# One queue for the planner's transfers, joint loads of q and k, and another source and time for the second weight matrix's sums

## The chip, the cores and the metric

The kernel runs on one core of one Trainium2 chip. The metric is the device time of one execution in microseconds (us), lower is better. TensorE (PE) multiplies matrices, VectorE (DVE) and ScalarE (ACT) work element by element, GpSimd (POOL) makes the maxima and sums over partitions. Transfers between the core's memory and DRAM are started by three of the queues: SP, which does nothing else, ACT, which also computes, and POOL. Each engine takes its instructions strictly in the order in which they stand. In the built program every transfer started by SP or ACT is given one of eight semaphores, in the order of the program and over both queues together; before it is started, the transfer that had the same semaphore last must have landed. A queue that waits for that also holds what stands behind it.

## The reference

Attention over 8 batches, 8 heads and 576 positions, each query seeing the 64 positions up to its own, and behind it a two-layer network (leaky slope 0.01) on the 4608 tokens:

```python
# q, k, v: (8, 8, 576, 64) float32; w_in: (512, 2048), w_out: (2048, 512)
scores = scale * np.matmul(q, k.transpose(0, 1, 3, 2))
mask = (rel >= 0) & (rel < 64)               # rel = query position - key position
scores = np.where(mask, scores, -1000000000.0)
attn = softmax(scores)
x = np.matmul(attn, v).transpose(0, 2, 1, 3).reshape(4608, 512)
h = x @ w_in
g = np.maximum(0.01 * h, h)
return g @ w_out
```

## The kernel before

Tokens are handled in pairs of 64-row query blocks, 36 pairs in all; `m` counts them. Every float32 product is made of three matmuls on a value's rounded part (hi) and what the rounding left (lo): hi*hi, hi*lo, lo*hi. The weights arrive as 64-bit numbers and become float32 on the chip. There are 32 half-tiles `n` (even: w_in, odd: w_out) for 16 tiles `f`; each goes through `raw` (a 512 KB load, L205, from ACT), `bits`, `sign`, `abs`, `clamp`, `join` (float32 in `singles[n]`), `chi` (`split`, L239: the hi part, and the float32 half-tile to DRAM, `w_single`, L241) and `rest` (the lo part, L245).

The work has three parts.

1. **The list** `ORDER` (L51 to 79), 0 to about 131 us. It is written out by hand: pairs 0 to 7, and the network's first products (`M`, L425, with `lk`, `gh`, `gl` for the leaky step and the split into hi and lo; `W`, L461) on the first 1024 tokens with tiles 0 to 7. All engines follow this one order. `ev` stores a finished sum.
2. **The walk**, about 131 to 357 us: the rest of the first 1536 tokens. 32 units `n`, each a product of 12 matmuls (L880), a leaky step (L894) and the cast to hi (L897) on ACT, the lo part on DVE (L900), and 12 matmuls into the sums (L889), which stand on PE two units behind the product. Beside it the pairs 8 to 19 are attended, the weights' raw parts are stored in DRAM (`store`, L632, 256 KB each), and sums of weight parts are prepared (`prepare`, L968) for the next part.
3. **The stages** `s` = 0, 1, 2, from 357 us, 1024 tokens each. The first layer is done in seven products in place of eight (`m`, L1058), for which `x_build` (L808) makes sums of attention rows and `prepare(0, ...)` sums of parts of w_in. The second layer is plain in stage 0 (`y`, L1083, in two halves) and in seven products in stages 1 and 2 (`z`, L1121). Weights come in 1 MB pieces on POOL's queue (`fill`, L1042) from two DRAM tensors, `w_first` and `w_second`. The last pairs, 20 to 35, are attended during stage 0 and at the start of stage 1.

From the walk on, the order is made by a planner, `arrange` (L524): each operation has an engine, an assumed duration, what it must come after, and a rank; the planner plays them through and notes the order in which they would start. `load` puts a transfer on SP, `bulk` puts one on ACT. The order on each engine is then fixed.

One pair's way through the engines: PE makes the scores (`S`, L272); DVE masks them (L657); POOL makes the maximum (L672); DVE subtracts it (L679); ACT takes the exponential (L683); POOL adds up (L675, 3.3 us each); a small transfer brings the sums to 128 partitions (`late_c`, L686, two of 2 KB); ACT adds a small number (`guard`, L690) and DVE inverts; two more transfers spread the inverse (`rows`, L697, and `late_r`, L710); DVE multiplies (`late_n`, L733); a last one stores the rows (`x_rows`, L736). q, k and v of a later pair are loaded by ACT (L161, L165, L169).

`prepare(n, f, ...)` loads parts of tiles f and f+8, makes sums and differences of their quarters (L979), splits them into hi (ACT, L982) and lo (DVE, L985), and stores them (L989 for w_out, into `w_second`; L992 for w_in, into `w_first`). Loads and stores of it stand on ACT:

```python
got = [bulk(partial(fetch, i), *freed, *all_in, rank=hurry + 0.1) for i in range(2)]
...
prepared[n, f] = [bulk(partial(keep, i), lo, rank=hurry + 0.1) for i in range(2)]
```

Finished sums leave the accumulators by copies that alternate between DVE and ACT (`early_out` L912, `put_out` L1086).

Of the kernel before, what the change touches and what calls it, by code (L numbers as in the profile page):

```python
# [38 lines left out]
PACE = 2  # L39
EARLY = 20  # L40
# [27 lines left out]
bits17 join16 sign17 L7 abs17 clamp17 join17 bits18 raw19 chi16 ev0 chi17 ev1 raw20 rest16 sign18 abs18 rest17 M11  # L68
bits19 clamp18 M12 lk11 gh11 gl11 lk12 gh12 sign19 join18 M13 W11 M14 gl12 abs19 raw21 chi18 lk13 bits20 clamp19
join19 chi19 raw22 sign20 rest18 rest19 W12 M15 gh13 gl13 abs20 W13 bits21 clamp20 sign21 join20 bits22 abs21 lk14  # L70
sign22 clamp21 join21 raw23 chi20 M16 gh14 gl14 W14 rest20 raw24 abs22 clamp22 join22 chi21 raw25 bits23 rest21 sign23
bits24 lk15 chi22 gh15 gl15 sign24 abs23 abs24 clamp23 join23 bits25 chi23 raw26 lk16 M17 W15 clamp24 sign25 rest22
join24 M18 abs25 gh16 raw27 clamp25 gl16 rest23 join25 W16 chi24 rest24 bits26 sign26 lk17 chi25 rest25 raw28 abs26
gh17 bits27 clamp26 gl17 sign27 join26 abs27 clamp27 join27 chi26 lk18 chi27 gh18 bits28 sign28 rest26 gl18 k8 q8 v8
W17 q9
# [27 lines left out]
def band_attention_ffn(ctx: ExitStack, tc: tile.TileContext, qT, kB, vW, vL, w_in, w_out, eye_mask, out, outT):  # L103
# [37 lines left out]
    qs = [const.tile([P, UNITS, NP, QB], F32, name=f"q{i}") for i in range(2)]  # L141
    ks = [const.tile([P, UNITS, NP, QB], F32, name=f"k{i}") for i in range(2)]
# [16 lines left out]
    def load_q(m, queue=nc.sync):  # L159
        if m < NU // 2:  # L160
            queue.dma_start(q_of(m), qT[m])  # L161

    def load_k(m, queue=nc.sync):
        if m < NU // 2:
            queue.dma_start(k_of(m), kB[m])  # L165
# [24 lines left out]
    w_single = dram.tile([2 * FT, P, 512], F32, name="w_single")  # L190
# [48 lines left out]
    def split(n):  # L239
        nc.scalar.copy(flat(parts(n)[0]), singles[n])  # L240
        nc.scalar.dma_start(w_single[n], singles[n])  # L241
# [238 lines left out]

    def idle(n):
        ps = bank("h", f"idle{next(count)}")
        for _ in range(n):
            nc.tensor.matmul(ps, wi[half + 4][0][:, 0], flat(wi[half + 4][0]), start=True, stop=True)

    def begin(k):
# [6 lines left out]
        ev=lambda k: due.pop(0)(),  # L493
    )
    nc.vector.memset(flat(wi[half + 4][0]).bitcast(F32), 0.0)
    nc.scalar.dma_start(k_of(0), kB[0])
# [24 lines left out]
    def bulk(fn, *after, rank=1.0):  # L521
        return op("ACT", 0.45, fn, *after, rank=rank, lag=1.5, land=6.0)

    def arrange():  # L524
# [9 lines left out]
        order = []  # L534
        while any(waiting.values()):
# [76 lines left out]
    for name in late.split():  # L612
# [3 lines left out]
        if kind == "raw":  # L616
            o["raw"] = bulk(partial(fetch_w, n), weights_of.get(n - 3, {}).get("join"), rank=0.2)
            continue
# [11 lines left out]

    def store(to, f, *cut):
        nc.sync.dma_start(to, both[f][cut])  # L632

    stored = []
    for f in turn_of:
        near, far = f % half, f // half
        for a, k in ((0, 0), (256, 4)) if far == 0 else ((256, 5),):
            to = first_at(near, k).rearrange("p (i c) -> p i c", i=2)
            stored.append((f, partial(store, to, f, slice(None), slice(2), slice(a, a + 256))))
        for a in range(2):  # L640
            to = second_at[:, (0, 2)[far] + (6, 2)[far] * a, near].rearrange("p (i c) -> p i c", i=2)
            stored.append((f, partial(store, to, f, slice(None), slice(2, 4), slice(256 * a, 256 * a + 256))))


# [63 lines left out]
    def spread_of(m, j):  # L708
        row = rows[m : m + 1, 512 * j : 512 * j + 512]
        nc.sync.dma_start(later["r"][64 * j : 64 * j + 64], row.broadcast_to([64, 512]))  # L710
# [41 lines left out]
    def attend(m, gate):  # L752

        o, late = at.setdefault(m, {}), 0.0 if early(m) else 0.5
        before, two, three = (at.get(m - i, {}) for i in (1, 2, 3))
        if m > PAIRED:
            if m > PAIRED + 1:
                o["q"] = bulk(partial(load_q, m, nc.scalar), two["S"], rank=0.5 + late)
            o["k"] = bulk(partial(load_k, m, nc.scalar), before["S"], rank=0.2 + late)
            o["v"] = bulk(partial(load_v, m, nc.scalar), before["X1"])  # L760
        takes = [before["take"], two["take"]] if m == EARLY else []
        if held_back(m - 1) and before:
            takes += [before["B0"], before["B1"]]
        o["S"] = op(
            "PE", 1.0, partial(scores_of, m), o.get("q"), o.get("k"), before.get("E1"), before.get("E0"), three.get("take"), *takes, s_free,
# [15 lines left out]
    def normalise(m):  # L781
# [11 lines left out]
        spread = [load(partial(spread_of, m, j), o["rows"], before.get("Y"), rank=0.3 + late) for j in range(2)]  # L793
# [21 lines left out]
    def x_build(s, n, xt_of, xt_free, x_free):  # L815
# [13 lines left out]
        def fetch(i):  # L829
            nc.sync.dma_start(xt_of()[0][:, 512 * i : 512 * (i + 1)], x_rows[m + i])  # L830

        got = [load(partial(fetch, i), *at[m + i]["kept"], *xt_free, rank=urge) for i in range(2)]
# [85 lines left out]
    def second_step(n):  # L918
# [5 lines left out]
        if n in ends:  # L924
            evicted[c] = []
            for i in range(4):
                engine = "DVE" if c == 1 or c == 0 and i < 2 or i % 2 == 0 else "ACT"
# [39 lines left out]
    def prepare(n, f, at, hurry, *freed):  # L967
        def prep(i):  # L968
            return (g_tile(at) if at else hold("spare", F32)).rearrange("p (k i c) -> p k i c", k=4, i=2)[:, :, i]
# [4 lines left out]
        def fetch(i):  # L974
            to = prep(0)[:, i::2] if n else prep(0)[:, 2 * i : 2 * i + 2]
            nc.scalar.dma_start(to, w_single[2 * (f + half * i) + n].rearrange("p (k c) -> p k c", k=2))
# [10 lines left out]
        def keep(i):  # L987
            if n:
                nc.scalar.dma_start(second_at[:, 1::2, f, 256 * i : 256 * i + 256], prep(i))  # L989
            else:  # L990
                a, b, k = ((0, 3, 1), (3, 4, 6))[i]
                nc.scalar.dma_start(  # L992
                    first_at(f, k, b - a), (g_tile(at) if at else hold("spare", F32))[:, 512 * a : 512 * b]
                )

        got = [bulk(partial(fetch, i), *freed, *all_in, rank=hurry + 0.1) for i in range(2)]
        d1 = op("DVE", 0.5, partial(join_of, 2, (0, 2), (0, 3), ALU.add), *got, rank=hurry, lag=2.0)
        d3 = op("DVE", 0.5, partial(join_of, 1, (0, 0), (0, 2), ALU.subtract), *got, rank=hurry, lag=2.0)
        d2 = op("DVE", 0.5, partial(join_of, 0, (1, 2), (0, 0), ALU.subtract), d1, rank=hurry)
        d4 = op("DVE", 0.5, partial(join_of, 3, (0, 1), (1, 0), ALU.subtract), d2, rank=hurry)  # L1000
        hi = op("ACT", 1.07, high, d1, d2, d3, d4, rank=hurry)
        lo = op("DVE", 1.4, low, hi, rank=hurry)
        prepared[n, f] = [bulk(partial(keep, i), lo, rank=hurry + 0.1) for i in range(2)]
# [6 lines left out]
    for f in range(half):  # L1010
        prepare(1, f, 0, OUT_PREP + 0.1 * f, *used_last[0])
# [73 lines left out]
    def put_out(s, t, i, o):  # L1085
        (nc.scalar.copy if i % 2 else nc.vector.tensor_copy)(o(), tiles[i])  # L1086
# [280 lines left out]
```

## Time and profile before

| | |
|---|---|
| median of 3 runs | 886.56 us (884.72 to 1079.68) |
| the profiled execution | 888.97 us, its span 887.2 us |
| weight load PEld busy | 690.0 us (78%), beside PE |
| DMA bytes over the span | 227.08 MB, mean 256 GB/s |
| of these on POOL's queue / ACT's / SP's | 90.18 / 77.31 / 58.51 MB |
| attention sums on POOL (L675) | 56 of 3.3 us |

A row of the timeline gives start, duration, engine, line, operation, output and inputs, how many instructions were merged, and in brackets the idle time just before and what ended it. ACTq and SPq are the queues' starts of transfers; a transfer's bytes move after that. PEclk is TensorE's granted clock as a share of full speed; "DMA" shares are of the sixteen DMA engines' time. The stretch table gives, for each stretch, its length, each engine's busy time with its count of instructions, PEclk, the DMA share and GB/s.

### The profile page before, as it was taken

Reading aid. Unit: us, or ns where it says so; the run is one execution under the profiler, and the core shown is the slowest. Engines: PE = TensorE matmul, PEld = TensorE weight load, DVE = VectorE, ACT = ScalarE, POOL = GpSimd, SP = SyncE. Lnnn points to the kernel's source line nnn. Section 1 sums busy time; section 2 is a strip of 40 time slices with the busy share of each in tenths; the row PEclk is TensorE's granted clock in tenths of the full one; section 3 lists DMA queues with packets and bytes.
Section 4 is the critical chain, followed back from the end, with each engine's and each line's share of the span. In section 5 each row is a group of like instructions: output and inputs, shape, how many; then the busy total and the mean of one; then the engine's idle time right before and its main releaser. Section 6 shows DMA issues by size and latency. Waiting matters only on the chain.

```text
span 887.2 us, 16927 instructions
## 1 busy us (share of the span) xinstructions
PE 853.5 (96%) x6778; PEld 690.0 (78%) x6778; DVE 631.6 (71%) x891; ACT 376.0 (42%) x620; POOL 364.2 (41%) x218
## 2 busy tenths in 40 slices
PE   8999999999999997999999899989999999999998
PEld 5776888888777776888887678767888888888886
DVE  7889885768579864875776989466578864545863
ACT  4655554333333333544453534253354523334431
POOL 5323000958768720677776777663000100000000
PEclk9999999999999998999999999989999999999999
DMA  9875876786899997799999998976856776666662
GB/s 342 265 233 184 275 219 240 234 302 207 276 292 336 314 317 273 245 299 356 309 295 317 295 300 266 344 235 207 276 195 214 236 242 210 194 191 197 199 222 87
DMA packets 103742, 227.08 MB, mean 256 GB/s; under 512 B 17008, under 2 KB 47856, under 8 KB 94704
## 3 DMA queue, kind: packets, MB, share of 16 engines
q0 software_dynamic: 14432, 90.18, 31.5%
q10 hardware_dynamic: 41712, 77.31, 26.3%
q1 hardware_dynamic: 47520, 58.51, 20.3%
q8 instruction: 53, 0.87, 0.4%
q14 instruction: 25, 0.20, 0.1%
HBM read 168.59 MB, written 57.26 MB: 255 GB/s over the span
## 4 chain that ended last, share of the span: by engine, by line
PE 48%; DMA 12%; DVE 9%; issue 3%; ACT 1%; SPq 1%; ACTq 0%; POOL 0%; DVEq 0%
PE m L1058 25%; PE z L1121 17%; DMA w_second<-p 2%; DMA late_r<-rows 2%; DMA w_second<-pspare 2%; DMA rows<-late_c 2%; DMA x_rows<-late_n 1%; PE y L1083 1%; PE acc L889 1%; DMA p<-x_rows 1%; PE s L272 1%; PE o L722 1%; DMA outT<-p 1%; DVE p L835 1%; DVE gs L1076 1%
## 5 line engine op out<-in xcount | busy, mean ns | idle before, releaser
L1058 PE MATMUL m<-pfew,p 128*128 128x512 f32 x720 | 171.5, 393 | 0.8 <-DVE pxa L1067 0.7
L1058 PEld LDWEIGHTS m<-pfew,p 128*128 128x128 f32 x720 | 134.8, 189 | 30.2 <-DVE pxa L1067 1.1
L1042 POOL DMA_DIRECT2D p<-w_second x44 | 26.3, 597 | 143.0 <-PE z L1121 98.8
L889 PE MATMUL acc<-p,gs 128*128 128x512 f32 x324 | 79.8, 394 | 0.0
L1042 POOL DMA_DIRECT2D p<-w_first x42 | 22.8, 542 | 134.0 <-PE m L1058 78.6
L1058 PE MATMUL m<-pxb,p 128*128 128x512 f32 x288 | 72.1, 397 | 5.0 <-ACT p L1070 5.0
L672 POOL PARTITION_ALL_REDUCE g<-late_f x20 | 37.0, 1894 | 96.1 <-DVE late_f L657 71.6
L675 POOL PARTITION_ALL_REDUCE late_o<-late_f x20 | 65.5, 3283 | 20.5 <-ACT late_f L683 12.3
L1067 DVE TENSOR_TENSOR p<-m,pxa 128x512 f32<-128x512 f32 x60 | 41.3, 688 | 41.9 <-PE m L1058 41.6
L1067 DVE TENSOR_TENSOR pxa<-m,pxa 128x512 f32<-128x512 f32 x60 | 41.3, 689 | 41.0 <-PE m L1058 38.0
L889 PEld LDWEIGHTS acc<-p,gs 128*128 128x128 f32 x324 | 60.1, 188 | 13.0
L1070 ACT ACTIVATE p<-p 128x512 f32<-128x512 f32 x60 | 37.9, 631 | 74.2 <-DVE p L1067 74.1
L1058 PEld LDWEIGHTS m<-pxb,p 128*128 128x128 f32 x288 | 54.4, 191 | 17.3 <-ACT p L1070 5.4
L880 PE MATMUL h<-pxa,p 128*128 128x512 f32 x228 | 58.4, 405 | 5.9 <-DVE gs L900 5.9
L675 POOL PARTITION_ALL_REDUCE late_o<-late_e x18 | 58.9, 3292 | 12.5 <-ACT late_e L683 8.0
L675 POOL PARTITION_ALL_REDUCE late_o<-e x18 | 58.8, 3285 | 8.2 <-ACT e L683 5.7
L1121 PE MATMUL z<-gs,p 128*128 128x512 f32 x240 | 57.6, 389 | 0.0
L880 PEld LDWEIGHTS h<-pxa,p 128*128 128x128 f32 x228 | 43.9, 195 | 16.5 <-DVE gs L900 7.2
L1083 PE MATMUL y<-gs,p 128*128 128x512 f32 x192 | 48.7, 406 | 3.8 <-issue 3.8
L1121 PEld LDWEIGHTS z<-gs,p 128*128 128x128 f32 x240 | 45.0, 188 | 9.4
L1121 PE MATMUL z<-third,p 128*128 128x512 f32 x216 | 51.9, 389 | 0.0
L1121 PE MATMUL z<-pxa,p 128*128 128x512 f32 x216 | 51.9, 389 | 0.0
(192 smaller groups left out, 1710.2 us busy)
## 6 DMA issues: line engine op xcount, KB each, us to landing
p<-w_second POOLq DMA_DIRECT2D x44, 1024.0 KB, 5.3
p<-w_first POOLq DMA_DIRECT2D x42, 1024.0 KB, 6.1
w_single<-w ACTq DMA_DIRECT2D x32, 256.0 KB, 4.4
w_second<-pspare ACTq DMA_DIRECT2D x16, 512.0 KB, 6.0
raw<-w_out ACTq DMA_DIRECT2D x15, 512.0 KB, 4.4
k<-kB ACTq DMA_DIRECT2D x28, 256.0 KB, 4.7
raw<-w_in ACTq DMA_DIRECT2D x14, 512.0 KB, 4.3
more_v<-vL ACTq DMA_DIRECT2D x14, 512.0 KB, 4.4
```

The costliest lines, as they stand in the source:

```text
L272: nc.tensor.matmul(ps[j][t, c : c + QB], k[i][s, p], q[s, w, p], start=not begun and (not more or (w, p) == (0, 0)), stop=not begun and no ...
L672: nc.gpsimd.partition_all_reduce(most_of(j), e_of(m)[:, j], P, ReduceOp.max)
L675: nc.gpsimd.partition_all_reduce(sum_of(j), e_of(m)[:, j], P, ReduceOp.add)
L722: nc.tensor.matmul(ps[64 * j : 64 * j + 64, c : c + QB], v[:, 2 * p + j], e_of(m)[:, j, c : c + QB], start=True, stop=True,)
L880: nc.tensor.matmul(ps, a[:, k, :], b[:, k], start=i == 0, stop=i == len(terms) - 1)
L889: nc.tensor.matmul(acc[c, i], a[:, i * P : (i + 1) * P], b, start=begin and k == 0, stop=n in ends and k == 2)
L1042: nc.gpsimd.dma_start(to, of)
L1058: nc.tensor.matmul(tiles[b], w[:, 256 * i + 128 * kt : 256 * i + 128 * kt + 128], x_part(OF_X[k], j, kt), start=begin and c == 0, stop=c = ...
L1067: nc.vector.tensor_tensor(to(), tiles[b], x(), ALU.add)
L1070: nc.scalar.activation(to(), to() if b is None else tiles[b], AF.Prelu, alpha=0.01)
L1083: nc.tensor.matmul(tiles[i], a, b, start=f == 0 and k == 0, stop=f == FT - 1 and k == 2)
L1121: nc.tensor.matmul(tiles[b + i], a, x, start=begin and f == 0 and c == 0, stop=f == half - 1 and c == 2, skip_group_check=not begin,)
```

## The change

- **Queues.** `bulk` is gone. From the walk on, every transfer that ACT started for the planner is started by SP: k, q and v, the loads and stores of `prepare`. Only the four last `raw` loads and the stores of `w_single` stay on ACT. The planner now also knows that SP can have eight transfers under way (`LANES`).
- **Joint transfers.** q and k lie beside each other in one DRAM tensor and one tile. From pair 10 on they come in one load of 512 KB; it waits for the scores of the pair before, where q alone waited for those of two pairs before. `late_r` is one transfer instead of two, two pairs' `x_rows` come in one load.
- **w_out's sums** are made of the stored raw parts: `prepare(1, f)` loads hi and lo of both tiles from `w_second` (1 MB in one load, before 512 KB of `w_single` in two), and DVE adds them (`whole_of`, 8 times on 128x1024) before the rest. `w_single` then needs only w_in: `split` stores every second half-tile, 16 stores fewer. The results go out in one store of 1 MB, before two of 512 KB.
- **Early stores.** The raw parts of tiles 0 to 7, 32 stores of 256 KB, are written in the list (`st0` to `st7`), before in the walk. 24 stores stay in the walk.
- **Copies out of the accumulators** that add nothing (L912, L1086) all stand on ACT, before every second one on DVE.

```diff
+LANES = 8
 bits17 join16 sign17 L7 abs17 clamp17 join17 bits18 raw19 chi16 ev0 chi17 ev1 raw20 rest16 sign18 abs18 rest17
-M11 bits19 clamp18 M12 lk11 gh11 gl11 lk12 gh12 sign19 join18 M13 W11 M14 gl12 abs19 raw21 chi18 lk13 bits20 clamp19
+st0 M11 bits19 clamp18 M12 lk11 st1 gh11 gl11 lk12 gh12 sign19 st2
+join18 M13 W11 M14 gl12 st3 abs19 raw21 chi18 lk13 bits20 st4 clamp19 join19 chi19 raw22 sign20 st5 rest18 rest19 W12
+M15 gh13 st6 gl13 abs20 W13 bits21 clamp20 st7 sign21 join20 bits22 abs21 lk14 sign22 clamp21 join21 raw23 chi20 M16
...
+    def load_qk(m):
+        nc.sync.dma_start(both_qk[m % 2], qk[m])
...
     def split(n):
         nc.scalar.copy(flat(parts(n)[0]), singles[n])
-        nc.scalar.dma_start(w_single[n], singles[n])
+        if n % 2 == 0:
+            nc.scalar.dma_start(w_single[n // 2], singles[n])
...
+    def stores_of(f):
+        near, far = f % half, f // half
+        todo = []
+        for a, k in ((0, 0), (256, 4)) if far == 0 else ((256, 5),):
+            to = first_at(near, k).rearrange("p (i c) -> p i c", i=2)
+            todo.append(partial(store, to, f, slice(None), slice(2), slice(a, a + 256)))
+        for a in range(2):
+            to = second_at[:, (0, 2)[far] + (6, 2)[far] * a, near].rearrange("p (i c) -> p i c", i=2)
+            todo.append(partial(store, to, f, slice(None), slice(2, 4), slice(256 * a, 256 * a + 256)))
+        return todo
...
-    def bulk(fn, *after, rank=1.0):
-        return op("ACT", 0.45, fn, *after, rank=rank, lag=1.5, land=6.0)
...
+            if e == "SP":
+                t = max(t, landed.pop(0))
             free[e] = t + x["us"]
             x["end"] = free[e] + x["land"]
+            if e == "SP":
+                landed.append(x["end"])
...
+    stored = [(f, fn) for f in turn_of if f >= half for fn in stores_of(f)]
...
+        if m > PAIRED + 1:
+            o["k"] = load(partial(load_qk, m), before["S"], rank=0.2 + late, land=6.0)
+        elif m > PAIRED:
+            o["k"] = load(partial(load_k, m), before["S"], rank=0.2 + late, land=6.0)
         if m > PAIRED:
-            if m > PAIRED + 1:
-                o["q"] = bulk(partial(load_q, m, nc.scalar), two["S"], rank=0.5 + late)
-            o["k"] = bulk(partial(load_k, m, nc.scalar), before["S"], rank=0.2 + late)
-            o["v"] = bulk(partial(load_v, m, nc.scalar), before["X1"])
+            o["v"] = load(partial(load_v, m), before["X1"], rank=0.3 + late, land=6.0)
...
-            (nc.scalar.copy if i % 2 else nc.vector.tensor_copy)(o, acc[c, i])
+            nc.scalar.copy(o, acc[c, i])
...
+            if n:
+                nc.sync.dma_start(tile_of().rearrange("p (k c) -> p k c", k=4), second_at[:, ::2, f])
...
+        def whole_of():
+            nc.vector.tensor_tensor(prep(0), prep(0), prep(1), ALU.add)
...
+        if n:
+            got = [op("DVE", 1.3, whole_of, *got, rank=hurry, lag=2.0)]
...
-        (nc.scalar.copy if i % 2 else nc.vector.tensor_copy)(o(), tiles[i])
+        nc.scalar.copy(o(), tiles[i])
```

Line numbers from here on are those of the kernel before, but for the rows of the changed kernel. Three places show what moves.

**ACT at the end of the walk.** `h` is a unit's product (leaky step, then cast to `gs`), `pxb` and `pfew` are x_build's casts, `late_c` is the guard. Before:

```order
L897 CAST gs_81<-h_7_3448 128x512
L690 ACTIVATE late_c_1789<-late_c_1789 128x8
L976 DMA pspare_1804<-w_single 128x2x256 x2
L992 DMA w_first<-p_24_2971 128x1536
L992 DMA w_first<-p_24_2971 128x512
L894 ACTIVATE h_8_3490<-h_8_3490 128x512
L992 DMA w_first<-p_23_2883 128x1536
L992 DMA w_first<-p_23_2883 128x512
L854 CAST pxb_3457<-p_26_3088 128x2x256
L897 CAST gs_82<-h_8_3490 128x512
```

In the changed kernel:

```order
L905 CAST gs_81<-h_7_3419 128x512
L902 ACTIVATE h_8_3481<-h_8_3481 128x512
L862 CAST pxb_3427<-p_26_3113 128x2x256
L862 CAST pfew_3447<-p_26_3113 128x256
L905 CAST gs_82<-h_8_3481 128x512
L862 CAST pfew_3447<-p_26_3113 128x4x256
```

The six transfers between the casts of units 7 and 8 are gone from ACT; the guard stands earlier.

**SP in the list.** The rows from the last load of k of the first eight pairs to the loads of pair 8. Before:

```order
L165 DMA k_86<-kB 128x512
L472 DMA sum_0_1248<-e 128x512
L472 DMA sum_1_1253<-e 128x512
L165 DMA k_85<-kB 128x512
L161 DMA q_83<-qT 128x512
L169 DMA v<-vL 128x2x512
L161 DMA q_84<-qT 128x512
```

In the changed kernel the first of 32 stores:

```order
L165 DMA qk_84<-qk 128x512
L476 DMA sum_0_1238<-e 128x512
L476 DMA sum_1_1242<-e 128x512
L497 DMA w_first<-pfew_85 128x2x256 x2
L497 DMA w_second<-pfew_85 128x2x256 x2
L497 DMA w_first<-pfew_85 128x2x256 x2
L497 DMA w_second<-pfew_85 128x2x256 x2
```

The stores stand between the two sums and the loads of pair 8; in the whole program's order the raw loads 21 to 25 of ACT stand among them.

**DVE at the end of stage 0's first half of y.** `y_0_0` to `y_0_3` are the four accumulators. Before:

```order
L857 TENSOR_TENSOR pxb_3457<-p_37_4079,pxb_3457 128x2x256
L733 TENSOR_TENSOR late_n<-o_4952,late_r 128x4x2x64
L1086 COPY p_26_3088<-y_0_0_4698 128x512
L1076 TENSOR_TENSOR pxa_38_4710<-pxa_34_3744,pxa_38_4710 128x512
L1086 COPY p_24_2971<-y_0_2_4713 128x512
```

In the changed kernel, on ACT:

```order
L1091 CAST pxa_38_4616<-pxa_34_3664 128x512
L1104 COPY p_26_3113<-y_0_0_4610 128x512
L1104 COPY p_26_3113<-y_0_1_4641 128x512
L1104 COPY p_24_2966<-y_0_2_4647 128x512
L1104 COPY p_24_2966<-y_0_3_4652 128x512
L1091 CAST pxa_38_4616<-pxa_34_3664 128x512
```

The copy of the first accumulator, on which the second half's first matmul waits, stood behind two DVE operations of other work; now all four stand in a row on ACT.

More of the change, by code (lines that the diff above doesn't have):

```diff
@@ L102, in band_attention_ffn @@
 @with_exitstack
-def band_attention_ffn(ctx: ExitStack, tc: tile.TileContext, qT, kB, vW, vL, w_in, w_out, eye_mask, out, outT):
+def band_attention_ffn(ctx: ExitStack, tc: tile.TileContext, qk, vW, vL, w_in, w_out, eye_mask, out, outT):
     nc = tc.nc
@@ L616, in band_attention_ffn @@
         if kind == "raw":
-            o["raw"] = bulk(partial(fetch_w, n), weights_of.get(n - 3, {}).get("join"), rank=0.2)
+            o["raw"] = op("ACT", 0.45, partial(fetch_w, n), weights_of.get(n - 3, {}).get("join"), rank=0.2, lag=1.5, land=6.0)
             continue
@@ L764, in attend @@
         o["S"] = op(
-            "PE", 1.0, partial(scores_of, m), o.get("q"), o.get("k"), before.get("E1"), before.get("E0"), three.get("take"), *takes, s_free,
+            "PE", 1.0, partial(scores_of, m), o.get("k"), before.get("E1"), before.get("E0"), three.get("take"), *takes, s_free,
             before.get("S"), rank=0.5 + late, lag=LAG if early(m) else 2 * LAG,
@@ L792, in normalise @@
                 at[m + 2][f"c{j}"]["after"].append(o["rows"])
-        spread = [load(partial(spread_of, m, j), o["rows"], before.get("Y"), rank=0.3 + late) for j in range(2)]
+        spread = [load(partial(spread_of, m), o["rows"], before.get("Y"), rank=0.3 + late)]
         if early(m):
@@ L926, in second_step @@
             for i in range(4):
[L927 removed]
+                engine = "DVE" if c == 1 or c == 0 and i < 2 else "ACT"
                 evicted[c].append(op(engine, 0.75, partial(early_out, c, i), seconds[n][i], *reloads[c], rank=0.1))
@@ L1009, in band_attention_ffn @@
         used_last[n] = prepared[0, f]
-    for f in range(half):
-        prepare(1, f, 0, OUT_PREP + 0.1 * f, *used_last[0])
+    for n, f in enumerate((4, 5, 6, 7, 0, 1, 2, 3)):
+        prepare(1, f, 0, OUT_PREP + 0.1 * n, *used_last[0])
         used_last[0] = prepared[1, f]
```

87 lines of the change are left out of this document (39 added, 48 removed).

## The prediction

> **What bounds the kernel now.** I read the page's busy shares first, then the slices with TensorE's clock, then stretches around the slices in which PE or its clock dips, then the timeline there, and last the chain of waits, which says what each stop waited for.
>
> ```profile
> span 887.2 us, 16927 instructions
> ...
> PE 853.5 (96%) x6778; PEld 690.0 (78%) x6778; DVE 631.6 (71%) x891; ACT 376.0 (42%) x620; POOL 364.2 (41%) x218
> ...
> PEclk9999999999999998999999999989999999999999
> ```
>
> PE is busy 96% of the span and the change touches none of its matmuls, so all there is to win is PE's idle time, 887.2 - 853.5 = 33.7 us, and the clock that dips behind stops. The stretches (us, their length, PE's busy time and instructions, the granted clock, the DMA share, GB/s) say where that lies:
>
> ```profile
> 0.00:80.00 80.00, 71.89 (x983) 1.00 0.79 266
> 92.00:131.00 39.00, 39.00 (x174) 1.00 0.80 261
> 240.00:337.30 97.30, 86.64 (x794) 0.99 0.96 321
> 337.30:357.00 19.70, 19.66 (x116) 0.87 0.73 241
> 480.00:503.30 23.30, 22.12 (x239) 1.00 0.93 296
> 503.30:520.00 16.70, 12.92 (x72) 0.80 0.96 294
> 560.00:575.70 15.70, 15.61 (x151) 1.00 1.08 372
> 575.70:600.00 24.30, 19.32 (x161) 0.86 0.74 234
> 600.00:620.00 20.00, 19.28 (x112) 1.00 0.66 204
> 860.00:887.20 27.20, 23.06 (x102) 0.96 0.31 104
> ```
>
> 8.1 us of the idle time lie in the first 80 us, 4.1 in the tail; the change reaches neither. Three single stops stand out in the timeline, and the clock is low behind each:
>
> ```profile
> 337.35 5.43 PE L880 MATMUL h<-pxa,p 128*128 128x512 f32 x12 [5.91 <-DVE gs L900]
> ...
> 507.10 4.18 PE L1083 MATMUL y<-gs,p 128*128 128x512 f32 x9 [3.78 <-issue]
> ...
> 580.68 2.93 PE L1058 MATMUL m<-pxb,p 128*128 128x512 f32 x6 [4.99 <-ACT p L1070]
> ```
>
> The clock's loss is busy time x (1 - PEclk) of the stretch: 19.66 x 0.13 = 2.6, 12.92 x 0.20 = 2.6, 19.32 x 0.14 = 2.7 us. So the three cost 5.9 + 2.6 = 8.5, 3.8 + 2.6 = 6.4 and 5.0 + 2.7 = 7.7, together 22.6 us. [...]
>
> **The two stops that stand behind transfers on ACT.** The chain of waits (start, length, what) at both places:
>
> ```profile
> 321.19 13.34 DMA w_second<-p
> ...
> 334.55 0.33 ACTq L992
> ...
> 335.99 0.59 ACT gs L897
> ...
> 336.60 0.70 DVE gs L900
> ...
> 569.41 9.16 DMA outT<-p
> ...
> 578.59 0.34 ACTq L165
> ...
> 579.61 1.02 ACT p L1070 x2
> ```
>
> ACT stood at a store of `prepare` (L992), which could not be started before a store of SP's that had its semaphore; the cast behind it, then DVE's lo part, then PE's product came late. At 578.59 it is a load of k, held by a store of outputs, and the sums' halving (L1070) behind it. After the change ACT has no transfers from the walk on, so neither hold can stand there. I take 8.5 + 7.7 out, and put 1 us back at each place for what is late next: at 337 the lo part needs DVE, and `x_build`'s last operation ended only just ahead of the first `m`:
>
> ```profile
> 356.37 1.55 DVE L857 TENSOR_TENSOR pfew<-p,pfew 128x256 fp32r<-128x256 f32 x2
> ```
>
> It ends at 357.92, and PE starts `m` on the earlier ones at 357.42; if the units end 8 us sooner this chain becomes the next bound, so I give back 1 more us.
>
> **The stop at y's second half.** Timeline around it:
>
> ```profile
> 502.82 2.98 DVE L857 TENSOR_TENSOR pxb<-p,pxb 128x512 fp32r<-128x512 f32 x1
> 503.18 0.57 ACT L1086 COPY p<-y 128x512 f32<-128x512 f32 x1
> ...
> 505.72 0.68 DVE L733 TENSOR_TENSOR late_n<-o,late_r 128x512 f32<-128x512 f32 x1
> 506.32 0.67 DVE L1086 COPY p<-y 128x512 f32<-128x512 f32 x1
> ```
>
> PE's next matmul writes the accumulator that DVE empties at 506.32, behind two operations of other work; ACT's copy was there at 503.18. With all four on ACT in a row (0.57 each, started about 503.2) the first accumulator is free about 3 us sooner. 6.4 out, 1 back for the first copy's 0.6 us and the wait for it.
>
> **Smaller stops.** 240 to 337.3: 97.30 - 86.64 - 5.91 = 4.7 us; 480 to 503.3: 1.2; 600 to 620: 0.7: 6.6 us together, with several causes. Between none and all of it goes; I take half, 3.3.
>
> **Stores in the list.** 32 stores of 256 KB, 8.4 MB, now stand before 131 us, where PE has no idle time at all (39.00 of 39.00), so this part can only lose. ACT's `raw` loads stand among them in program order and share their semaphores:
>
> ```profile
> 117.66 0.45 ACTq L205 DMA_DIRECT2D raw<-w_in  x1
> 118.21 0.60 ACT L430 ACTIVATE g<-h 128x512 f32<-128x512 f32 x1 [0.31 <-ACT p L240]
> ...
> 124.97 2.88 PE L425 MATMUL h<-pxb,p 128*128 128x512 f32 x12
> ...
> 92.00:118.00 26.00, 26.00 (x117) 21.52 (x116) 20.44 (x38) 15.21 (x26) 0.00 (x0) 1.00 0.85 280
> ```
>
> Before that `raw` load 26 us x 280 GB/s = 7.3 MB went; with the stores that stand ahead of it, and half of the `w_single` stores less, it is about 13.5 MB. At 372 GB/s (the busiest stretch) that takes 36 us, 10 more than before; at 321 (240 to 337) 42 us, 16 more. The leaky step behind it on ACT ended 118.81, and PE's product that needs its room came at 124.97: slack 6.2. The slip is then 4 us by the first rate, 10 by the second, and none if the stores slip in beside; I take 4, since the stretch reached a share of 0.80 and has room up to the busiest one's rate. The walk has 32 stores less on SP for it, which the row of 0.96 share (240 to 337.3) says is worth something; it is in the 3.3 above.
>
> **w_out's sums, and fewer copies on DVE.**
>
> ```profile
> L1110 DVE TENSOR_TENSOR p<-p,p 128x1024 f32<-128x1024 f32 x12 | 16.9, 1406 | 0.2
> ...
> L1086 DVE COPY p<-y 128x512 f32<-128x512 f32 x4 | 2.6, 678 | 0.0
> ...
> 480.00:560.00 80.00, 71.48 (x86) 0.96 0.91 284
> ```
>
> `whole_of` is 8 x 1.41 = 11.2 us of DVE; seven copies leave it, 7 x 0.68 = 4.8 us; net +6.4. DVE in stage 0 is busy 71.48 of 80, so 8.5 us are free there and most of it hides; if it did not, 6 us at worst. `prepare(1, f)`'s loads grow from 512 KB to 1 MB, 8 x 0.5 = 4.2 MB, in a stretch at 0.91 DMA share; the halved `w_single` stores (16 x 256 KB = 4.2 MB) give that back in the list. I take 1 us (0 to 6). Joint loads of q and k, one `late_r` for two and the 1 MB result stores remove starts of 0.3 to 0.5 us from queues that wait on landings: nothing, as long as SP still has idle time.
>
> **One queue.** Counted in the two programs, SP goes from 322 transfers to 384, ACT from 179 to 47. Each pair passes three small transfers in series, and they now stand behind loads of 512 KB and 1 MB. Landings of the first (`late_c`), min/median/max, and what ACT's guard waited once:
>
> ```profile
> DMA to landing us min/median/max: 1.6/4.9/9.0
> ...
> 569.26 0.21 ACT L690 ACTIVATE late_c<-late_c 128x8 f32<-128x8 f32 x1 [5.08 <-DMA late_r<-rows]
> ```
>
> A landing already varies from 1.6 to 9.0 us, so a step can lose up to 7 us or gain 3 (4.9 to 1.6). The planner places the guard late enough for the median; I take nothing, as the total traffic is the same, and leave the rest to the rivals. [...]
>
> **Sum.** 22.6 + 3.3 - 3 (1 us at each place) - 1 (`x_build`) = 21.9 out; 4 + 1 = 5 in; net -17. The profiled execution took 888.97, 2.4 above the median 886.56; it would come to 872, the median to 869. By its own terms' bounds this case runs from 860 to 877.
>
> **Rivals.**
> - *Nearly all stops go and the list does not slip.* The stores fit into SP's idle time of the list at 0.80 DMA share. 22.6 + 6.6 - 2 = 27 out: 859. Against it: PE had no idle time there to absorb anything.
> - *The holds move.* SP, now with all loads and stores in one row, holds k, v and `x_rows` behind stores as ACT's were, and PE stops elsewhere: one of three stops saved (7.5 each) less the list's 4: 883. For it: SP started nothing for 9 us just ahead of the 337 stop, though it had work:
>
> ```profile
> 326.06 0.33 SPq L736 DMA_DIRECT2D x_rows<-late_n  x1
> ...
> 335.32 1.49 SPq L710 DMA_DIRECT2D late_r<-rows  x2
> ```
>
>   That the stops were none of ACT's queue's doing would end here too.
> - *Slower: the pairs' small transfers wait for bulk.* Place: `late_c`, `rows` and `late_r` on SP, then the guard in ACT's order and the casts behind it. A 1 MB piece ahead at 372 GB/s costs 2.8 us; on every second of 28 pairs 1.4 x 28 = 39, less the 22 that the stops give: 17 slower, 904. It takes the gain from 22 / 28 = 0.8 us a pair on, and is slower by 2% from 1.4. For it: 0.91 to 0.96 DMA share in the stages' first half. Against it: the pairs are attended well ahead of their use.
>
> **How the numbers follow.** Forecast 0.50, all stops gone 0.20, holds moved 0.15, small transfers late 0.15. 2% of 886.56, about what a measurement of this kernel tells from no change, is 17.7: 868.8 and 904.3. Half of the forecast's 0.50 lies below 868.8: faster 0.25 + 0.20 = 0.45. Slower: the greater part of the last rival with the list's worst, 0.11. Within 2%: 0.44. The range reaches from 853 (all stops gone with 29.2 out and a little more from the walk's lighter SP) to 890, which takes in the moved holds and leaves out the last rival and little more.
>
> **What would show it.** No starts of transfers on ACT from the walk on; no stop over 2 us at the walk's end, at y's second half and in the first 20 us of stage 1, and PEclk 0.95 or more there; in 92 to 131 a DMA share near 1 and PE idle 4 us; `late_c`'s landing median near 5. The forecast is wrong if PE stops with `late_c` L696 (the guard) or a held SP as releaser in the chain, or if the list ends more than 11 us later.

## The result, and the profile after

| | time, us | ratio to before, 95% interval |
|---|---|---|
| before, on the same chip | 888.84 (median) | |
| the changed kernel | 974.58 (median of 4: 973.40 to 982.76) | 1.1001 [1.0912, 1.1091] |

Slower by 86 us; 869 was forecast. Some executions are over 1.5% above the fastest of the same kernel, such as one of before at 1079.68 us and three of the four of a3 below; the ratios leave them out, the medians do not, and a3 keeps one run, 973.52 us, and has no ratio.

The page of the changed kernel: the span, the busy shares, the granted clock, and the lines that hold most of the chain that ended last.

```profile
span 971.6 us, 16819 instructions
...
PE 874.5 (90%) x6778; PEld 704.5 (73%) x6778; DVE 622.5 (64%) x892; ACT 378.2 (39%) x627; POOL 367.4 (38%) x218
...
PEclk9999999989999997999789999989999999999999
...
PE m L1076 18%; PE z L1139 16%; DMA late_r<-rows 15%; DMA rows<-late_c 6%; DMA late_c<-late_o 4%; PE h L888 3%; PE acc L897 3%; DMA p<-x_rows 2%; PE h L429 2%; PE acc L465 2%; PE s L276 1%; POOL late_o L681 1%; DMA outT<-p 1%; POOL g L678 1
```

PE does the same 6778 instructions. Its idle time went from 33.7 to 971.6 - 874.5 = 97.1 us, and the lower clock (0.956 in place of 0.987) makes its work 21 us longer; together that is the whole difference of the spans. Every engine's share fell, so none of them is the new bound. A quarter of the chain is now the three transfers that a pair passes in series (15 + 6 + 4%). The stretch of the last pairs (length; PE, PEld, DVE, ACT and POOL busy; clock, DMA share, GB/s), before:

```profile
450.00:560.00 110.00, 105.04 (x1042) 84.27 (x1041) 93.58 (x112) 44.95 (x81) 80.43 (x44) 0.97 0.92 289
```

and after:

```profile
450.00:560.00 110.00, 84.16 (x821) 66.97 (x822) 59.77 (x81) 34.08 (x64) 63.89 (x34) 0.89 0.76 244
```

The DMA engines moved less, 244 GB/s in place of 289: the transfers came late though there was room. The list of who waited for the tile `late_r` (us in all, times) has, before:

```profile
  DVE late_n L733: 1.2, 1
```

and after:

```profile
  DVE late_n L738: 98.8, 18
```

The timeline of the changed kernel at the end of the walk shows how one such wait reaches PE:

```profile
366.54 0.69 DVE L738 TENSOR_TENSOR late_n<-late_n,late_r 128x512 f32<-128x512 f32 x1 [16.29 <-DMA late_r<-rows]
...
367.63 0.62 ACT L862 CAST pxb<-p 128x512 fp32r<-128x512 f32 x1 [17.28 <-DMA p<-x_rows]
...
368.46 0.58 ACT L905 CAST gs<-h 128x512 fp32r<-128x512 f32 x1
...
369.75 0.68 DVE L908 TENSOR_TENSOR gs<-h,gs 128x512 fp32r<-128x512 f32 x1
...
370.49 2.07 PE L888 MATMUL h<-pxa,p 128*128 128x512 f32 x4 [12.59 <-DVE gs L908]
```

DVE stands 16.29 us at a pair's product; the walk's lo part is behind it on DVE, and PE's next product behind that. `late_r` had been started at 354.83, so 11.7 us passed before its data was there. It is not the only late transfer on this path: ACT stood 17.28 us for a load of `x_rows`, started at 355.45, and the unit's cast to hi (L905), which the lo part needs too, is behind that; it ended at 369.04, only 0.7 us before the lo part started. Without DVE's wait this one would have held PE nearly as long.

### The profile page after: what moved, and what is told of

It reads as the page before. It is cut to its first block, busy times and chain, and to the rows that moved or that the text cites. A ratio compares the mean times of both kernels' runs of the same rounds, so it can differ in the third digit from the quotient of the medians.

```text
span 971.6 us, 16819 instructions
## 1 busy us (share of the span) xinstructions
PE 874.5 (90%) x6778; PEld 704.5 (73%) x6778; DVE 622.5 (64%) x892; ACT 378.2 (39%) x627; POOL 367.4 (38%) x218
## 4 chain that ended last, share of the span: by engine, by line
PE 47%; DMA 34%; DVE 9%; issue 4%; POOL 3%; ACT 1%; SPq 1%; ACTq 0%; DVEq 0%; POOLq 0%
PE m L1076 18%; PE z L1139 16%; DMA late_r<-rows 15%; DMA rows<-late_c 6%; DMA late_c<-late_o 4%; PE h L888 3%; PE acc L897 3%; DMA p<-x_rows 2%; PE h L429 2%; PE acc L465 2%; PE s L276 1%; POOL late_o L681 1%; DMA outT<-p 1%; POOL g L678 1%; DMA more_v<-vL 1%
## 5 line engine op out<-in xcount | busy, mean ns | idle before, releaser
L897 PE MATMUL acc<-p,gs 128*128 128x512 f32 x324 | 82.4, 401 | 0.0
L1076 PE MATMUL m<-pxb,p 128*128 128x512 f32 x288 | 74.7, 408 | 6.9 <-ACT p L1104 6.5
L1060 POOL DMA_DIRECT2D p<-w_second x44 | 26.3, 597 | 139.0 <-PE z L1139 98.8
L888 PE MATMUL h<-pxa,p 128*128 128x512 f32 x228 | 60.7, 416 | 15.4 <-DVE gs L908 15.4
L1076 PEld LDWEIGHTS m<-pxb,p 128*128 128x128 f32 x288 | 56.4, 198 | 20.5 <-ACT p L1104 6.9
L1085 DVE TENSOR_TENSOR pxa<-m,pxa 128x512 f32<-128x512 f32 x60 | 41.3, 689 | 33.7 <-PE m L1076 31.4
L1101 PE MATMUL y<-gs,p 128*128 128x512 f32 x192 | 54.2, 432 | 0.0
```

Source lines behind the costliest of these rows:

```text
L888: nc.tensor.matmul(ps, a[:, k, :], b[:, k], start=i == 0, stop=i == len(terms) - 1)
L897: nc.tensor.matmul(acc[c, i], a[:, i * P : (i + 1) * P], b, start=begin and k == 0, stop=n in ends and k == 2)
L1060: nc.gpsimd.dma_start(to, of)
L1076: nc.tensor.matmul(tiles[b], w[:, 256 * i + 128 * kt : 256 * i + 128 * kt + 128], x_part(OF_X[k], j, kt), start=begin and c == 0, stop=c = ...
L1085: nc.vector.tensor_tensor(to(), tiles[b], x(), ALU.add)
L1101: nc.tensor.matmul(tiles[i], a, b, start=f == 0 and k == 0, stop=f == FT - 1 and k == 2)
```

## The experiments

The runs came in four groups; each has its own runs of the kernel before, whose medians lay between 887.1 and 889.8 us. What separated the theories first was a number of the trace: from the start of `late_r` (of its second half where there are two) to the product that uses it, the shortest of 28 pairs took 4.05 us before and 8.00 after, and the mean went from 8.8 to 11.6.

**First group: the form of late_r, the queues, the stores.** a1 takes the changed kernel and puts `late_r` back into two transfers:

```diff
-        nc.sync.dma_start(later["r"], rows[m].rearrange("(j c) -> j c", j=2)[:, None].broadcast_to([2, 64, 512]))
+        for j in range(2):
+            row = rows[m : m + 1, 512 * j : 512 * j + 512]
+            nc.sync.dma_start(later["r"][64 * j : 64 * j + 64], row.broadcast_to([64, 512]))
```

> The changed kernel with late_r (the spread of a pair's inverse sums) in two transfers of 64 rows each, as before, both started by one step of the plan so that the order stays. Theory F (the form of late_r: in the changed kernel no multiplication by it starts less than 8.0 us after its start, against 4.0 before; the joint transfer itself lands slowly): the mean from late_r's start to late_n falls from 11.6 to 9 us or less, and the time falls by 30 us or more, to 945 or less. Theory Q (everything in one queue: small transfers stand behind bulk loads whatever their form): mean stays at 11, the time stays within 10 us of 974.6. Theory S (the 32 stores in the list): no change here.

b1 makes only the opposite edit, in the kernel before (its `spread` list then has one load).

> The kernel before with late_r alone made one transfer for both halves; ACT's queue, loads and stores as before. Theory F: the time rises by 20 us or more from 888.8, and no late_n starts less than 7.5 us after late_r's start. Theory Q: within 5 us of before, since bulk is still on the other queue. Theory S: no change.

a3 takes the changed kernel and gives ACT its transfers back:

```diff
+    def bulk(fn, *after, rank=1.0):
+        return op("ACT", 0.45, fn, *after, rank=rank, lag=1.5, land=6.0)
...
-        nc.sync.dma_start(both_qk[m % 2], qk[m])
+        nc.scalar.dma_start(both_qk[m % 2], qk[m])
...
-        got = [load(partial(fetch, i), *freed, *all_in, *written, rank=hurry + 0.1, land=6.0 + n) for i in range(2 - n)]
+        got = [bulk(partial(fetch, i), *freed, *all_in, *written, rank=hurry + 0.1) for i in range(2 - n)]
...
-        prepared[n, f] = [load(partial(keep, i), lo, rank=hurry + 0.1, land=6.0 + n) for i in range(2 - n)]
+        prepared[n, f] = [bulk(partial(keep, i), lo, rank=hurry + 0.1) for i in range(2 - n)]
```

> The changed kernel with the loads of q, k and v and the loads and stores of prepare started by ACT again; late_r stays joint, early stores, joint q and k and the sums from stored parts stay. Theory Q: the time falls by 50 us or more, to 925 or less, and the guard's waits for late_c (59 us in 14 waits) fall under 20. Theory F: it falls by less than half of the 86 us, to 935 or more, because late_r still lands late. Theory S: stays at 975.

a4 takes `st0` to `st7` out of the changed kernel's list:

```diff
-    stored = [(f, fn) for f in turn_of if f >= half for fn in stores_of(f)]
+    stored = [(f, fn) for f in turn_of for fn in stores_of(f)]
```

> The changed kernel with the 32 stores of tiles 0 to 7 put back from the list to the walk. Theory S: the time falls by 5 us or more, PE's idle time in 80 to 131 us goes from 4.9 to under 1. Theories F and Q: only that first stretch gains, at most 6 us, and the walk loses some of it, since SP then has 32 starts more beside the pairs: 965 to 985.

| run | time, us | ratio to before, 95% interval |
|---|---|---|
| a1, late_r in two | 893.96 | 1.0039 [1.0007, 1.0072] |
| b1, late_r joint, nothing else | 968.75 | 1.0866 [1.0780, 1.0953] |
| a3, bulk on ACT | 973.52 (the three others 989.45 to 990.80) | none given |
| a4, no early stores | 975.37 | 1.0957 [1.0884, 1.1030] |

The form of this one transfer carries about 80 of the 86 us, in both directions: a1 takes 81 away, b1 puts 79 on. From `late_r` to the product, a1 has 3.35 us at the least and 8.4 in the mean, b1 7.98 and 12.4, as theory F expected. Bulk on SP's queue does not carry it: with ACT's queue back the time did not fall. Nor do the early stores: in a4 PE's idle time from 80 to 131 us went from 4.9 to 0, and the time stayed. In a1 DVE's wait for `late_r` is

```profile
  DVE late_n L740: 24.3, 9
```

and in b1, where ACT still starts the bulk,

```profile
  DVE late_n L732: 82.4, 18
```

**Second group: what of the form.** The joint transfer differs in two ways: it is one of 256 KB, and its source begins with a dimension of 2. a5 has two transfers of 128 KB that each begin with 2:

```diff
+        for i in range(2):
+            c = slice(256 * i, 256 * i + 256)
+            row = rows[m].rearrange("(j c) -> j c", j=2)[:, c]
+            nc.sync.dma_start(later["r"][:, c], row[:, None].broadcast_to([2, 64, 256]))
```

> The changed kernel with late_r again in two transfers of 128 KB, but each covers all 128 rows and half of the columns, so that its source still begins with a dimension of 2. Theory F2 (what makes late_r slow is that leading dimension: the transfer is spread over few of the sixteen DMA engines): as slow as the changed kernel, 955 to 995. Theory F1 (it is slow because it is one transfer of 256 KB where there were two of 128): as fast as with two of 64 rows, 885 to 905.

a6 keeps one transfer of 256 KB, but stores the sums eight times, so that the source begins with 16:

```diff
-        nc.sync.dma_start(rows[m].rearrange("(p b) -> p b", b=8), later["c"][m % 2])
+        for j in range(2):
+            to = rows[m, 8 * j : 8 * j + 8].rearrange("r (p b) -> p r b", b=8)
+            nc.sync.dma_start(to, later["c"][m % 2][64 * j : 64 * j + 64][:, None].broadcast_to([64, 8, 8]))
...
+        nc.sync.dma_start(later["r"], rows[m][:, None].broadcast_to([16, 8, 512]))
```

> The changed kernel with late_r as one transfer of 256 KB, but the inverse sums stored eight times in DRAM (two transfers of 16 KB for rows where one of 4 KB was), so that the source begins with a dimension of 16, each repeated for 8 rows. Theory F2: fast, 890 to 910, with at most 10 us lost by the larger rows transfers; late_n's waits for late_r fall from 98.8 us to under 40. Theory F1: as slow as the changed kernel, 955 or more.

a62 is the same with two copies, so the source begins with 4 (`broadcast_to([4, 32, 512])`).

> The same with the inverse sums stored twice: the source begins with 4, each repeated for 32 rows. Theory F2: between the two, nearer to the fast one if the time of a transfer goes as one over the engines: 895 to 935. Theory F1: 955 or more.

a13 is a1 and a3 together.

> The changed kernel with late_r in two transfers of 64 rows and, beside that, the loads of q, k, v and the loads and stores of prepare on ACT's queue again. With late_r mended alone it took 893.96. If the move to SP is worth what was forecast (22 us of stops at ACT's transfers and the clock behind them), this takes 905 or more; if the move is worth nothing, 885 to 900; if small transfers on SP suffer from the bulk there (theory Q), under 885.

| run | source of late_r begins with | time, us | ratio to before, 95% interval |
|---|---|---|---|
| a5, two by columns | 2 | 982.91 | 1.1041 [1.0951, 1.1131] |
| the changed kernel | 2 | 974.58 | 1.1001 [1.0912, 1.1091] |
| a62, rows twice | 4 | 929.32 | 1.0439 [1.0353, 1.0525] |
| a6, rows eight times | 16 | 906.04 | 1.0161 [1.0089, 1.0233] |
| a1, two of 64 rows | 64 | 893.96 | 1.0039 [1.0007, 1.0072] |
| a13, two of 64 rows, bulk on ACT | 64 | 887.22 | 0.9994 [0.9960, 1.0028] |

a13 is 7 us under a1 where the forecast's worth of the move to SP would have put it 11 above: the move brings nothing here.

The time follows the leading dimension, not the number or size of the transfers: it falls from 2 (982.91 and 974.58 us) to 4 (929.32), 16 (906.04) and 64 (893.96).

The kept traces show the spread itself, in the packets of SP's queue. The last joint `late_r` of the changed kernel was started at 696.45, just behind 256 KB of `x_rows`; both are 128 packets of 2 KB. Those of `x_rows` took 0.88 us (696.85 to 697.73), with up to 19 in flight. Those of `late_r` took 5.28 us (697.97 to 703.25) at 0.084 us each, with two in flight for 4.61 of it and never more than three. In the kernel before, the halves started at 622.56 and 623.06 had their 128 packets through in 1.61 us, with up to 18 in flight: 3.7 us less.

The traces also hold the time of every step by which a transfer's semaphore is counted up. In the kernel before each of the 615 transfers leaves 16 steps. In the changed kernel each of the 28 joint `late_r` leaves 3: one 0.9 to 1.6 us after its start, and two not before 7.0 us; the other 489 transfers leave 16. In a5 it is 3 as well, in a62 5 (one at 1.0 to 1.5 us, four not before 4.5), in a6 and a1 16. Without the early one they number 2 and 4 where the source begins with 2 and 4; where it begins with 16 or 64 they are 16. By the last step, a pair's `late_r` landed 7.1 us after its start at the least and 9.5 in the median, where both halves together took 3.3 and 5.9 before: 3.8 longer at the least, close to the 3.7 of the packets.

Why a6 is still 12 us above a1 was not settled; its rows transfers are eight times larger.

**Third group: whose lateness.** Is PE late because `late_r` is late, or because the other transfers are? a7 takes a1 and adds a transfer of 256 KB per pair in the joint form, to a place that nobody reads; a8 adds the same bytes in a form that begins with 128.

```diff
+        row = rows[m].rearrange("(j c) -> j c", j=2)[:, None].broadcast_to([2, 64, 512])
+        nc.sync.dma_start(unused[m].rearrange("(j p) c -> j p c", j=2), row)
```

```diff
+        nc.sync.dma_start(unused[m], rows[m : m + 1, :512].broadcast_to([P, 512]))
```

> The changed kernel with late_r in two transfers of 64 rows (893.96 us) and, behind them, one more transfer of 256 KB per pair in the joint form (source begins with 2), from DRAM to a place in DRAM that nobody reads. It tells whether the joint form hurts by its own lateness or by what it does to the others. Own lateness alone: within 10 us of the next kernel and under 910. Others too (the few DMA engines that it is on are kept busy, and every other transfer has a share on them): 20 us or more above the next kernel.

> The control: the same extra 256 KB per pair, in a form whose source begins with 128. Under both readings 890 to 910: 28 transfers of 0.26 MB are 7 MB on 227.

a7 took 986.23 us (1.1132 [1.1084, 1.1179]), a8 910.74 us (1.0280 [1.0244, 1.0316]). Nobody waits for the spare data, and still it costs 75 us more in the one form than in the other. The control is just above its range, 17 us above a1: the extra bytes have a price too. The guard's waits for `late_c`, 2 KB each and in the same form in all kernels, are in a7

```profile
  ACT late_c L697: 88.5, 15
```

and in a8

```profile
  ACT late_c L697: 26.6, 11
```

and the stretch 460 to 560 us, in a7

```profile
460.00:560.00 100.00, 79.47 (x747) 61.87 (x746) 54.99 (x73) 30.65 (x55) 60.51 (x33) 0.95 0.85 284
```

and in a8

```profile
460.00:560.00 100.00, 92.00 (x959) 73.91 (x958) 80.06 (x97) 40.74 (x77) 73.39 (x39) 0.97 0.98 322
```

So a transfer in the joint form holds up the others: the guard waits 88.5 us for `late_c` in place of 26.6, while the DMA engines' mean share in this stretch is 0.85 in place of 0.98. The steps of the semaphores say how. In a8 a `late_c` has fourteen of its sixteen steps 4.9 us after its start, and both others 0.7 us later (medians of 56). In a7 the fourteen are there after 4.1 us, and both others 3.0 us later; one transfer, started at 503.15, has fourteen after 5.2 us and the last two after 12.2 and 12.4. So fourteen steps come no later than in a8, and two come late, as many as a joint `late_r` leaves behind its early one. In the changed kernel it is the same: 1.7 us for the last two of `late_c` in place of 0.3 before, and 4.3 for those of the 512 KB loads of v in place of 0.6 or less. That the late two are on the very engines of the narrow transfer is the author's reading of their number and was not shown: the trace doesn't name the engine.

One rival is that the late transfer keeps its semaphore and so holds SP. In the trace of the kernel before, the 529 transfers of SP and ACT use eight semaphores, and none starts before the one ahead of it on its semaphore has landed. But SP's waits for the spare transfer come to 8.5 us in all in a7 and 0.3 in a8: at most a small part of the 75.

**Third and fourth group: where the forecast gain went.** With `late_r` mended the change was still 4 us slower than before. a14 is a1 without the early stores; b2 is the kernel before with only the copies on ACT:

```diff
-            (nc.scalar.copy if i % 2 else nc.vector.tensor_copy)(o, acc[c, i])
+            nc.scalar.copy(o, acc[c, i])
...
-        (nc.scalar.copy if i % 2 else nc.vector.tensor_copy)(o(), tiles[i])
+        nc.scalar.copy(o(), tiles[i])
```

> The changed kernel with late_r in two and the 32 stores of tiles 0 to 7 back in the walk. If the list's 7 us (its first walk matmul at 140.4 against 133.1) come from the stores and the walk can carry them, 885 to 889; if the walk loses as much by them as the list gains, 892 to 897.

> The kernel before with nothing but the copies out of the accumulators (early ones and those of y) all on ACT. If the stop at y's second half goes without another taking its place, 882 to 885 (6.4 us less 1, from the forecast); if the planner's order gives it back elsewhere, 886 to 893.

c1 to c4 each add one other part of the change to b2. c1 is the queues: `bulk` becomes a load on SP, and the planner gets `LANES`.

```diff
     def bulk(fn, *after, rank=1.0):
-        return op("ACT", 0.45, fn, *after, rank=rank, lag=1.5, land=6.0)
+        return load(fn, *after, rank=rank, land=6.0)
```

> The kernel before with the copies on ACT (873.28 us), and of the rest of the change only the queues: q, k, v and prepare's loads and stores on SP, eight under way in the planner. If the move costs time by itself (pairs' small transfers behind bulk in one queue), 880 to 900. If the stops at ACT's transfers were worth what was forecast, 860 or less. If neither, 868 to 880.

c2 is the joint load, on ACT:

```diff
-                o["q"] = bulk(partial(load_q, m, nc.scalar), two["S"], rank=0.5 + late)
-            o["k"] = bulk(partial(load_k, m, nc.scalar), before["S"], rank=0.2 + late)
+                o["k"] = bulk(partial(load_qk, m), before["S"], rank=0.2 + late)
```

> The same base with only the joint load of q and k, on ACT's queue, from the pair before's scores on. If the later, larger load is what PE waits for in the changed kernels (2 to 5 us at a time at the scores), 880 to 890; if the planner hides it, 868 to 878.

c3 is the changed `prepare` with its order of the eight parts and the halved `w_single`, on ACT's queue; c4 is `stores_of`, the list with `st0` to `st7`, and 24 stores in the walk. Their diffs are those of the change.

> The same base with only the sums of w_out made from the stored raw parts (8 more operations of 1.4 us on DVE, 1 MB loads, half of the w_single stores), on ACT's queue. By the forecast's term 1 us more (0 to 6): 870 to 880. If it is where the change gives its gain back, 882 or more.

> The same base with only the 32 stores of tiles 0 to 7 written in the list. By the forecast's term 4 us more (0 to 11), less what the walk gains: 873 to 884, with the walk's first matmul 4 to 8 us later than at 130.6; if the walk gains nothing, 880 or more, if it gains as much, 870 to 875.

| run | time, us | ratio to before, 95% interval |
|---|---|---|
| a14, late_r in two, no early stores | 896.32 | 1.0117 [1.0069, 1.0164] |
| b2, copies on ACT alone | 873.28 | 0.9838 [0.9805, 0.9871] |
| c1, b2 and the queues | 871.44 | 0.9812 [0.9771, 0.9853] |
| c2, b2 and joint q and k | 887.67 | 0.9973 [0.9942, 1.0005] |
| c3, b2 and sums from parts | 885.59 | 0.9935 [0.9893, 0.9977] |
| c4, b2 and early stores | 880.38 | 0.9906 [0.9863, 0.9950] |

By the ratios, the copies alone make the kernel 14 us faster. Against b2, the queues change nothing that can be measured; joint q and k cost 12 us, sums from parts 9, early stores 6, each give or take 4 to 5 us. None of these steps reaches 2%. The parts don't add: 12 + 9 + 6 = 27, and a1, with all of them and the queues, is 18 above b2.

b2's expectation, 882 to 893, missed: it took 873. a14 fell into its second range, the walk losing what the list gained: the walk's first product starts at 128.64 us in place of a1's 140.42, but PE stopped 11.51 us at 341.69 in the walk. c1 came out in the range for neither effect, c2 and c3 in their dearer ranges. c4's time is in its range. b2 and c1 beat both kernels; between them nothing is decided.

The page of b2:

```profile
span 868.9 us, 16945 instructions
...
PE 849.5 (98%) x6778; PEld 688.7 (79%) x6778; DVE 618.9 (71%) x884; ACT 378.3 (44%) x627; POOL 362.8 (42%) x218
...
PEclk9999999999999999999999999999999999999999
```

No slice is left with a low clock, and PE is idle 868.9 - 849.5 = 19.4 us: all three stops are gone, also the two behind ACT's transfers, though ACT has all its transfers still. One other stands in the trace, 4.22 us at 512.58 before a pair's product with v.

c4's list (stretch with the engines as above, then the timeline of ACT and PE):

```profile
92.00:131.00 39.00, 33.64 (x134) 26.75 (x134) 20.03 (x38) 14.24 (x25) 0.00 (x0) 0.91 1.06 366
```

```profile
120.77 0.60 ACT L429 ACTIVATE g<-h 128x512 f32<-128x512 f32 x1 [3.32 <-DMA w_second<-p]
...
121.42 2.07 PE L424 MATMUL h<-pxb,p 128*128 128x512 f32 x4 [4.84 <-ACT g L429]
```

The DMA share is over 1 and ACT stands behind a landing of one of the stores: the mechanism of the forecast. The walk's first product starts at 144.36 us in place of b2's 130.59, and the first `m` at 354.93 in place of 346.38. The expectation of 4 to 8 us for the walk's start missed.

## Why the prediction was wrong

- **The step that failed** is the sentence on the joint transfers: "Joint loads of q and k, one `late_r` for two and the 1 MB result stores remove starts ... nothing". The joint `late_r` costs about 80 us, shown both ways by a1 and b1, by its own lateness and by holding up other transfers (a7's spare one, which nobody reads, costs 75 us more than a8's). It was priced by its starts alone; its form, an outermost dimension of 2 where there were 64 rows, was in the diff. The range could not hold a cost that stood in the sum as nothing.
- **The rival "small transfers wait for bulk"** named the right transfers and the right path, `late_c`, `rows` and `late_r` before the guard and before DVE's product, but the wrong cause. Bulk on the same queue is not it: c1 moves it there and stays at b2's time. c1's `late_c` landed in a median of 5.3 us against b2's 4.3, and that cost no time that can be measured.
- **Two stops behind transfers on ACT** (8.5 + 7.7 us): the chain of waits read them rightly for that run, but taking them for what the queue costs was wrong. b2 loses them with the queues as they were, and c1, which takes them off ACT, is no faster than b2. The stops belonged to one order of the plan; a new order moves them. In a1 the walk's stop is gone (PE busy 120.00 of 120.00 from 240 to 360), but the one at stage 1 is there again, now behind the guard in ACT's order (PE's next `m` starts at 575.29 after 5.95 us of idle time, behind the copies of L1106):

```profile
563.13 0.47 SPq L692 DMA_DIRECT2D late_c<-late_o  x1
...
574.55 0.21 ACT L696 ACTIVATE late_c<-late_c 128x8 f32<-128x8 f32 x1 [5.95 <-DMA late_c<-late_o]
574.67 2.03 ACT L1106 COPY p<-y 128x512 f32<-128x512 f32 x4
```

- **The copies on ACT**: forecast 6.4 - 1 for y's second half; measured 14 alone. The stop at y's second half is gone in b2 as forecast, though c2, with the same copies on ACT, has one there again. That the new order took the other two stops with it was not forecast of the copies; that part is luck.
- **The stores in the list**: mechanism right. 4 forecast (0 to 10); in the changed kernel the walk's first product starts 5.6 us later (138.70 against 133.12), near the forecast. In c4, which has all the `w_single` stores still, it is 14, of which the walk gave 5 back; 6 net by the ratios.
- **w_out's sums**: 1 forecast (0 to 6), 9 measured. That DVE's free time would hide it was wrong; c3's longest stop is one of 8.36 us at 335.78 in the walk, where PE waits for DVE's lo part. Why the order puts it there was not followed further.
- **Joint q and k**: forecast at nothing, 12 measured. PE's stops in c2 are not at the scores as expected, but at y and m behind ACT's copies (4.04 us at 508.98, 5.83 at 571.21); whether the load or the other order of the plan brings them stays open.
- **Two slips of the working** carry nothing: in the trace of the kernel before ACT starts 207 transfers, not 179; and with every term at its worst (no smaller stop gained, 10 for the list, 6 for w_out's sums) the sum's own bound is 884, not 877.

## What to carry to other kernels

Two transfers made one were far dearer here than two: look at the leading dimension that the joint one gets. A 2 cost about 80 us, 4 about 35 and 16 about 12, measured from two transfers that begin with 64 and, for 4 and 16, with larger `rows` transfers in it. What the narrow transfer cost did not show in who read it, since other transfers waited too: a7's spare copy, which nobody reads, took 75 us more than a8's, and such a copy is a test for that. And where a planner fixes the order, a stop seen in one profile is not the price of the thing it waits for: test each part of a change alone before summing.

## What was not expected of the hardware

- A transfer of 256 KB per pair that begins with 2 costs the kernel 75 us more over 28 pairs than one of the same bytes that begins with 128, 2.7 us a pair, though nothing needs its data (a7, a8).
- Fourteen of the sixteen steps of another transfer's semaphore come in time then, and the last two 3.0 us later (`late_c` in a7; 0.7 in a8).
- In the changed kernel the mean DMA share fell (0.92 to 0.76 in 450 to 560 us) while DVE's waits for `late_r` rose (1.2 to 98.8 us over the whole run): the low share did not mean that the transfers were in time.
- The granted clock followed PE's stops: 0.89 in that stretch, and PE's unchanged work took 874.5 us in place of 853.5. In the kernel before it stood at half for 6.8 us at each of the three stops.
